# 180 identity products without readers at low priority, and two PSUM banks in place of four for the first attention

## The chip, the cores and the metric

The kernel runs on one core of a Trainium2 chip. The metric is the device time of one execution in microseconds (us). Engines are named as in the profile: PE is the matrix engine, PEld its weight loads, DVE the vector engine, ACT the scalar engine, POOL the GpSimd engine, and SP the engine whose queue issues most DMAs.

## The reference

```
def sm_attn(qq, kk, vv):
    s = scale * np.matmul(qq, kk.transpose(0, 1, 3, 2))
    s = s - np.max(s, axis=-1, keepdims=True)
    a = np.exp(s)
    a = a / (np.sum(a, axis=-1, keepdims=True) + 1e-09)
    return np.matmul(a, vv)
p_packed = sm_attn(p, k, v)
out = sm_attn(q, p_packed, p_packed)
...
h = x @ w_in
sp = np.maximum(h, 0.0) + np.log1p(np.exp(-np.abs(h)))
g = h * erf(sp)
return (g @ w_out).astype(np.float32)
```

There are 8 batches of 8 heads, 576 tokens and a head size of 64. 32 packed queries attend to all tokens (first attention step), and all tokens then attend to the 32 packed results (second step). The outputs, 4608 tokens of 512 features, go through a gated layer with 2048 hidden features. w_in (512 x 2048) and w_out (2048 x 512) arrive as 64-bit floats.

## The kernel before, in words

**Attention per batch.** `attention(b)` is a generator of 12 stages. It loads p, k, v and q of a batch, computes the first scores (L165, tiles s), their maximum and exponential (L170, L174), normalizes (L179), transposes the attention with identity products (L186 and L192, tiles t and p), multiplies with v (L198) and copies the packed result to `pt` (L203). The second scores (L212) are transposed and normalized on DVE and ACT (L215 to L229) and split into a high part `a2h` (ACT, L232) and a low part `a2l` (DVE, L233). Attention of batch b+1 runs beside the units of batch b.

**Folded weights.** `w_prime(b, j)` multiplies `pt` with a quarter of w_in (L243), and ACT and DVE write the product as a high and a low part, `wph` (L245) and `wpl` (L246). So the hidden features need no product of their own with the attention output.

**Units.** A unit is half the tokens of a batch (c = 0 or 1) and one of 8 blocks of 256 hidden features (i). `h_block` makes the hidden block with 12 products of 128x288 into two banks of PSUM (L264; pool `ps_h` with two buffers), copies it with ACT (L267), and passes it through ACT and DVE in turn: L270, L271, L272 on ACT, L273 and L274 on DVE, L275 on ACT, and on DVE the last product, which gives `g` (L280). `o_block` runs three units later (LAG = 3) and adds g times w_out into four PSUM banks, `ps_o0` to `ps_o3` (L308). In the first 12 units (WHOLE) g is one 32-bit tile and each product with w_out is written once; later it is split in parts. A product of two 32-bit tiles counts as two instructions on PE in the profile.

**Weights in 64 bits.** `load_f32` turns a 128x512 piece of w_in or w_out into 32 bits: a DMA into a staging tile (L83, 512 KB), one pass of ACT (L87) and three of DVE (L88, L89, L90). The staging pool has two buffers, and only six conversions (EARLY) borrow others. The next DMA into a staging buffer is issued when the last pass of DVE over it is done. There are 32 such pieces; `plan` spreads them over the first units, and half of w_in and w_out (16 pieces) fall into the first attention and the first five units.

**What sets the order.** The instructions of each engine are put in order when the kernel is built, by a scheduler with modelled durations. What stands earlier in the program has the higher priority. On the chip each engine runs its list strictly in that order, and waits on semaphores where an input isn't there. In names of tiles with their numbers, h0_0_1_0 is batch 0, half 0, block 1, first of its two banks; hs, t, u and g carry batch, half and block; wos4 is the staging tile of piece 4 of w_out and wo4 the converted piece; wi2_3 is the staging tile of quarter 2 of w_in, piece 3.

**Banks of the first attention.** The attention of batch 0 runs before any unit, so the o banks are free. With `roomy` set, `bank` (L125 to L132) goes round three places: `ps_o0` and `ps_o1`, then `ps_o2` and `ps_o3`, then the shared place `ps_m`. Its pieces in turn are the first scores of both halves of the tokens, the transposes t, the packed result p and the second scores of both halves.

Of the kernel before, what the change touches and what calls it, by code (L numbers as in the profile page):

```python
# [8 lines left out]
F32 = mybir.dt.float32  # L9
# [19 lines left out]
def tile_pack_attention_moe(ctx: ExitStack, tc: tile.TileContext, qT, kT, v, pT, w_in, w_out, outT):  # L29
    nc = tc.nc  # L30
    P = 128
    B, _, NC, S = qT.shape
# [17 lines left out]
    WI_AT = (-1, 1)  # L50
    ATT1 = (0, 2)
    ATT2 = 14
    CONV = 2

    EARLY = ("wpl", "wpl", "wph", "wph", "wpl", "wpl")
# [7 lines left out]
    ps_o = ctx.enter_context(tc.tile_pool(name="ps_o", bufs=1, space=bass.MemoryType.PSUM))  # L63
# [3 lines left out]
    ident = cpool.tile([P, P], F32, name="ident")  # L67
# [24 lines left out]
    def load_w_in(j, c, **slot):  # L92
        load_f32(w_in_sb[:, c, j * FB:(j + 1) * FB], w_in[c * P:(c + 1) * P, j * FB:(j + 1) * FB], f"wi{j}_{c}", **slot)

    def load_w_out(f, **slot):
        made = opool.tile([P, DM], F32, name=f"wo{f}", tag="wo")
        load_f32(made[:], w_out[f * P:(f + 1) * P, :], f"wos{f}", **slot)
        wo[f] = made

    def split_w_out(f):  # L100
        hi = opool.tile([P, DM], F32R, name=f"woh{f}", tag="wo")
        lo = opool.tile([P, DM], F32R, name=f"wol{f}", tag="wo")
        nc.scalar.copy(hi[:], wo[f][:])
        nc.vector.tensor_tensor(lo[:], wo[f][:], hi[:], op=ALU.subtract)
        wo_hi[f], wo_lo[f] = hi, lo
# [8 lines left out]
    def attention(b, roomy=False):  # L114
# [3 lines left out]
        turn = [0]  # L118
# [6 lines left out]
        def bank(name):  # L125

            turn[0] += 1
            if roomy and turn[0] % 3:
                d = turn[0] % 3 * 2 - 2
                return [ps_o.tile([P, 512], F32, name=f"{name}_{b}_{x}", tag=f"ps_o{d + x}")[:] for x in range(2)], None  # L130
            ps = ps_m.tile([P, 2, 512], F32, name=f"{name}_{b}", tag="ps_m")
            return [ps[:, 0, :], ps[:, 1, :]], ps  # L132

# [17 lines left out]
        for j in range(NCH):  # L151
            n = min(P, S - j * P)
# [8 lines left out]
        for c2 in range(2):  # L161
            banks = bank(f"s1_{c2}")
            for c in range(NC):
                for r in range(2):
                    nc.tensor.matmul(banks[0][r][NK * c:NK * c + NK, 0:HT], p[64 * r:64 * r + 64, c, :],  # L165
                                     k[c][64 * r:64 * r + 64, c2 * HT:(c2 + 1) * HT], start=True, stop=True)
            copy_out(a1[:, :, c2 * HT:(c2 + 1) * HT], banks, HT)
            yield
# [11 lines left out]
        yield  # L180
        a1t = apool.tile([P, NCH, 2, P], F32, name=f"a1t{b}", tag="big")
        banks = bank("t1")
        for j in range(NT):
            for r in range(2):
                o = (j % 2 * 2 + r) * P
                nc.tensor.transpose(banks[0][j // 2][:, o:o + P], a1[:, r, j * P:(j + 1) * P], ident[:])  # L186
        copy_out(a1t[:, 0:NT].rearrange("p (x j) r k -> p x (j r k)", x=2), banks, 512)
        yield
        banks = bank("p")
        po, pr = banks[0]  # L190
        for r in range(2):
            nc.tensor.transpose(pr[0:REM, r * P:(r + 1) * P], a1[:, r, NT * P:S], ident[:])  # L192
        nc.scalar.copy(a1t[0:REM, NT].rearrange("p r k -> p (r k)"), pr[0:REM, 0:2 * P])
        for j in range(NCH):
            n = min(P, S - j * P)
# [41 lines left out]
    def w_prime(b, j):  # L237
        hi = wpool.tile([P, 2, FB], F32R, name=f"wph{b}_{j}", tag="wph")
        lo = wpool.tile([P, 2, FB], F32R, name=f"wpl{b}_{j}", tag="wpl")
        ps = ps_m.tile([P, 2, 512], F32, name=f"wp{b}_{j}", tag="ps_m")  # L240
        for c in range(NC):
            for r in range(2):
                nc.tensor.matmul(ps[NK * c:NK * c + NK, r, :], pt[b][64 * r:64 * r + 64, NK * c:NK * c + NK],  # L243
                                 w_in_sb[64 * r:64 * r + 64, c, j * FB:(j + 1) * FB], start=True, stop=True)
        nc.scalar.copy(hi[:], ps[:])  # L245
        nc.vector.tensor_tensor(lo[:], ps[:], hi[:], op=ALU.subtract)  # L246
        wp[b, j] = (hi, lo)
# [46 lines left out]
    def o_block(b, c, i, first, last):  # L294

        g = gs.pop((b, c, i))
        t0 = b * S + c * HT
        if first:
            acc[b, c] = []
            for d in range(NDM):  # L300
                po = ps_o.tile([P, 512], F32, name=f"o{b}_{c}_{i}_{d}", tag=f"ps_o{d}")
                acc[b, c].append(po)
        for d in range(NDM):
            for k in range(2):
                f = 2 * i + k
                terms = [(wo, g[0])] if len(g) == 1 else [(wo_hi, g[0]), (wo_hi, g[1]), (wo_lo, g[0])]
                for n, (w, gg) in enumerate(terms):
                    nc.tensor.matmul(acc[b, c][d][:, 0:HT], w[f][:, d * P:(d + 1) * P], gg[:, k, :],  # L308
                                     start=(first and k == 0 and n == 0),
                                     stop=(last and k == 1 and n == len(terms) - 1))  # L310
        if not last:
            return
        for d in range(NDM):
            ob = tpool.tile([P, HT], F32, name=f"ob{b}_{c}_{i}_{d}", tag="ob", bufs=NDM)
            nc.scalar.copy(ob[:], acc[b, c][d][:, 0:HT])
            where = outT[d * P:(d + 1) * P, t0:t0 + HT]
            if (b, c) in begun:
                nc.gpsimd.dma_start(where, ob[:], accum_op=ALU.add)
            else:
                nc.sync.dma_start(where, ob[:])  # L320
        begun.add((b, c))
# [15 lines left out]
    def at(n):  # L337
        return plan.setdefault(n, [])
# [10 lines left out]
    for ph, lists in conv.items():  # L349
# [4 lines left out]
        else:  # L354
            flat = [it for items in lists for it in items]
            n0, n1 = (2 * NB0 * TURNS[p] for p in (ph - 1, ph))
            for k, it in enumerate(flat):
                at(n0 + CONV + k * (n1 - n0 - 2 * CONV) // len(flat)).append(it)
    ready, whole_w = {0: -1}, {}

    def plan_attention(b):
        free = last_of[b - 2] + 1 if b > 1 else 0
        start, end = ATT1 if b == 1 else (free, free + 6)
        if b == NB0 and b > 1:
            start, end = ATT2, first_use[b] - 2
        end = max(free, min(end, first_use[b] - 2))
# [10 lines left out]
    for k, (b, j) in enumerate(uses):  # L377
        if b not in ready:
            plan_attention(b)
        n = ready[b]  # L380
        if k >= NFB:
            n = max(n, last_use[uses[k - NFB]])
        n = max([n] + [m for m, its in plan.items() if any(it[0] == "wi" and it[1] == j for it in its)])
# [10 lines left out]
    def do(items):  # L394
        for it in items:
            if it[0] == "att":
                b = it[1]
                if b not in gens:
                    gens[b] = attention(b)
                next(gens[b])  # L400
            elif it[0] == "sp":
                split_w_out(it[1])
            elif it[0] in ("wi", "wo"):
                conversions[0] += 1
                slot = {}
                if 2 < conversions[0] <= 2 + len(EARLY):
                    slot = dict(pool=wpool, tag=EARLY[conversions[0] - 3])
                if it[0] == "wi":
                    load_w_in(it[1], it[2], **slot)
                else:  # L410
                    load_w_out(it[1], **slot)
            elif it[1:] == (0, 0):
                with tc.high_priority():
                    w_prime(0, 0)
            else:
                w_prime(it[1], it[2])

    first = attention(0, roomy=True)
    early = plan.pop(-1, [])
    next(first)  # L420
# [8 lines left out]
    for n in range(len(units) + LAG):  # L429
        if n < len(units):  # L430
            h_block(*units[n][:3], n < WHOLE)
            do(plan.pop(n, []))
        if n >= LAG:
            o_block(*units[n - LAG])

# [37 lines left out]
```

## Time and profile before

| | us |
|---|---|
| median of 3 runs | 792.65 (790.92 to 794.25) |
| the profiled execution | 789.89 |
| its span | 788.1 |
| PE busy | 744.6 (94%) |
| DVE busy | 599.7 (76%) |
| ACT busy | 597.6 (76%) |

The profiled execution has 1.8 us around its span. Times in a timeline are counted from the start of the span. A row of the timeline has start, duration, engine, line, operation, tiles (written from read), shape and count, and in brackets the idle time of the engine before it and what ended it. A row of the table of stretches has the stretch, its length, the busy time of PE, PEld, DVE, ACT and POOL with instruction counts, the granted clock of PE as a share of full speed, the DMA share and GB/s. The granted clock comes from records of its changes; before the first record, at 8.52 us, the table has no record and writes 1.00.

### The profile page before, as it was taken

The numbers are of one execution on the slowest core, as the hardware profiler recorded it, in microseconds if no ns is written. First come the engines' busy times: TensorE is split into PE (matmuls) and PEld (weight loads), VectorE is DVE, ScalarE is ACT, GpSimd is POOL, SyncE is SP. The second block draws the span as 40 slices with busy tenths as digits, with TensorE's granted clock in tenths as the row PEclk, the third lists the DMA queues.
The fourth block names the chain that finished last, engine by engine and source line by source line (L and its number), as shares of the span: only waits on it lengthen the run. The fifth ranks groups of instructions, "written<-read, shape, count | busy, mean of one in ns | idle before, by whom it ended". The sixth has DMA issues, their size and how long they took to land.

```text
span 788.1 us, 15219 instructions
## 1 busy us (share of the span) xinstructions
PE 744.6 (94%) x6256; PEld 664.1 (84%) x6256; DVE 599.7 (76%) x916; ACT 597.6 (76%) x1011; POOL 15.1 (2%) x22
## 2 busy tenths in 40 slices
PE   3549988999999999999999999999999999999998
PEld 2228756899998898899799998889888998899998
DVE  3887898977689678867887769767886769766664
ACT  3357778988689878887687868778687867878784
POOL 0000000000111100000000000000000000000000
PEclk8568999999999999999999999999999999999999
DMA  8834735002542422013200222002300210000000
GB/s 306 291 110 149 243 116 162 31 17 67 107 88 31 83 76 89 1 39 98 80 32 1 83 81 72 13 1 80 132 32 1 79 47 1 31 2 31 1 31 31
DMA packets 31813, 58.39 MB, mean 74 GB/s; under 512 B 3584, under 2 KB 14848, under 8 KB 31744
## 3 DMA queue, kind: packets, MB, share of 16 engines
q1 hardware_dynamic: 29440, 55.06, 21.5%
q0 software_dynamic: 2304, 2.36, 2.6%
q8 instruction: 49, 0.80, 0.4%
q14 instruction: 20, 0.16, 0.1%
HBM read 45.61 MB, written 11.80 MB: 73 GB/s over the span
## 4 chain that ended last, share of the span: by engine, by line
PE 82%; DVE 7%; DMA 6%; ACT 3%; issue 1%; SPq 0%; ACTq 0%
PE o L308 50%; PE h L264 24%; PE wp L243 4%; DMA wi<-w_in 4%; DMA wos<-w_out 2%; PE p L198 2%; PE s L212 1%; PE s L165 1%; PE t L186 1%; DVE w_in_sb L89 1%; ACT t L270 1%; DVE wo L89 1%; ACT wo L87 1%; DVE w_in_sb L90 1%; DVE g L280 0%
## 5 line engine op out<-in xcount | busy, mean ns | idle before, releaser
L308 PE MATMUL o<-gl,woh 128*128 128x288 f32 x928 | 273.3, 295 | 0.0
L308 PE MATMUL o<-gh,woh 128*128 128x288 f32 x928 | 273.1, 300 | 0.0
L308 PE MATMUL o<-gh,wol 128*128 128x288 f32 x928 | 272.9, 295 | 0.0
L308 PEld LDWEIGHTS o<-gh,woh 128*128 128x128 f32 x928 | 172.1, 187 | 25.5 <-DVE t L273 8.9
L308 PEld LDWEIGHTS o<-gl,woh 128*128 128x128 f32 x928 | 174.3, 188 | 1.8 <-issue 1.3
L308 PEld LDWEIGHTS o<-gh,wol 128*128 128x128 f32 x928 | 174.6, 188 | 1.5 <-issue 1.3
L267 ACT ACTIVATE hs<-h 128x288 f32<-128x288 f32 x256 | 103.2, 412 | 95.4 <-PE h L264 94.6
L264 PE MATMUL h<-a2h,wph 128*128 128x288 f32 x512 | 155.2, 304 | 10.6 <-ACT wph L245 5.9
L264 PE MATMUL h<-a2l,wph 128*128 128x288 f32 x512 | 152.7, 298 | 1.8 <-DVE a2l L233 1.8
L264 PE MATMUL h<-a2h,wpl 128*128 128x288 f32 x512 | 152.6, 298 | 0.0
L283 DVE SCALAR_TENSOR_TENSOR hs<-t,hs 128x576 f32<-128x576 f32 x116 | 87.7, 756 | 72.5 <-ACT t L275 72.5
L275 ACT ACTIVATE t<-t,bias 128x576 f32<-128x576 f32 x128 | 98.8, 772 | 25.3 <-DVE t L274 25.0
L264 PEld LDWEIGHTS h<-a2h,wph 128*128 128x128 f32 x512 | 97.2, 190 | 22.3 <-ACT wph L245 6.8
L273 DVE SCALAR_TENSOR_TENSOR t<-t,hs 128x576 f32<-128x576 f32 x128 | 95.9, 750 | 20.1 <-ACT u L272 19.8
L270 ACT ACTIVATE t<-hs,bias 128x576 f32<-128x576 f32 x128 | 99.6, 778 | 2.9
L271 ACT ACTIVATE t<-t,bias 128x576 f32<-128x576 f32 x128 | 99.3, 775 | 2.3
L264 PEld LDWEIGHTS h<-a2l,wph 128*128 128x128 f32 x512 | 97.4, 190 | 4.3 <-DVE a2l L233 2.8
L272 ACT ACTIVATE u<-t,bias 128x576 f32<-128x576 f32 x128 | 99.3, 776 | 1.8
L264 PEld LDWEIGHTS h<-a2h,wpl 128*128 128x128 f32 x512 | 97.3, 190 | 1.9 <-issue 1.9
L274 DVE SCALAR_TENSOR_TENSOR t<-u,t 128x576 f32<-128x576 f32 x128 | 96.3, 752 | 1.6
L287 DVE TENSOR_TENSOR gl<-hs,gh 128x576 fp32r<-128x576 f32 x116 | 87.3, 753 | 1.5
L286 DVE CAST gh<-hs 128x576 fp32r<-128x576 f32 x116 | 52.9, 456 | 35.0 <-PE o L308 33.8
(60 smaller groups left out, 637.3 us busy)
## 6 DMA issues: line engine op xcount, KB each, us to landing
k<-kT SPq DMA_DIRECT2D x32, 288.0 KB, 4.3
q<-qT SPq DMA_DIRECT2D x32, 288.0 KB, 4.3
outT<-ob SPq DMA_DIRECT2D x64, 144.0 KB, 1.8
wi<-w_in SPq DMA_DIRECT2D x16, 512.0 KB, 6.0
v<-v SPq DMA_DIRECT2D x32, 256.0 KB, 3.6
wos<-w_out SPq DMA_DIRECT2D x16, 512.0 KB, 3.6
outT<-ob POOLq DMA_DIRECT2D x16, 144.0 KB, 3.7
v<-v SPq DMA_DIRECT2D x8, 128.0 KB, 4.2
```

What stands on the lines that cost most here:

```text
L264: nc.tensor.matmul(ps[:, 0:HT], w[:, r, fo:fo + P], a[:, r, c * HT:(c + 1) * HT], start=(n == 0), stop=(n == 5))
L267: nc.scalar.mul(hs[:, k, :], ps[:, 0:HT], 0.5)
L270: nc.scalar.activation(t[:], hs[:], AF.Tanh, bias=bias[:, 0:1], scale=2.0 * T_SCALE)
L271: nc.scalar.activation(t[:], t[:], AF.Square, bias=bias[:, 1:2], scale=Q_SCALE)
L272: nc.scalar.activation(u[:], t[:], AF.Tanh, bias=bias[:, 2:3], scale=U_SCALE)
L273: nc.vector.scalar_tensor_tensor(t[:], t[:], 0.5 * A2, hs[:], op0=ALU.mult, op1=ALU.add)
L274: nc.vector.scalar_tensor_tensor(t[:], u[:], 0.5 * A1, t[:], op0=ALU.mult, op1=ALU.add)
L275: nc.scalar.activation(t[:], t[:], AF.Tanh, bias=bias[:, 3:4], scale=2.0 * A_SCALE)
L283: nc.vector.scalar_tensor_tensor(hs[:], t[:], 1.0, hs[:], op0=ALU.add, op1=ALU.mult)
L286: nc.vector.tensor_copy(ghi[:], hs[:])
L287: nc.vector.tensor_tensor(glo[:], hs[:], ghi[:], op=ALU.subtract)
L308: nc.tensor.matmul(acc[b, c][d][:, 0:HT], w[f][:, d * P:(d + 1) * P], gg[:, k, :], start=(first and k == 0 and n == 0), stop=(last and k = ...
```

## The change

There are two edits. `bank` goes round two places instead of three: `ps_o0` and `ps_o1`, then `ps_m`. And after the hidden block of unit 0 and the plan's work of that unit, `keep_busy` writes 180 products of the 128x128 identity with itself into a tile in `ps_o3`. Nothing reads that tile.

```
+    BUSY = 180
...
         def bank(name):
             turn[0] += 1
-            if roomy and turn[0] % 3:
-                d = turn[0] % 3 * 2 - 2
-                return [ps_o.tile([P, 512], F32, name=f"{name}_{b}_{x}", tag=f"ps_o{d + x}")[:] for x in range(2)], None
+            if roomy and turn[0] % 2:
+                return [ps_o.tile([P, 512], F32, name=f"{name}_{b}_{x}", tag=f"ps_o{x}")[:] for x in range(2)], None
...
+    def keep_busy():
+
+        idle = ps_o.tile([P, P], F32, name="idle", tag="ps_o3")
+        for _ in range(BUSY):
+            nc.tensor.matmul(idle[:], ident[:], ident[:], start=True, stop=True)
...
         if n < len(units):
             h_block(*units[n][:3], n < WHOLE)
             do(plan.pop(n, []))
+        if n == 0:
+            keep_busy()
         if n >= LAG:
             o_block(*units[n - LAG])
```

In the program the products stand behind the first attention and unit 0, and ahead of unit 1; the scheduler puts them into PE's list in ten groups. In PE's order they are: 13 ahead of the first scores, 36 ahead of the transposes t, 15 ahead of the products with v, 13 ahead of the second scores, 14 ahead of the first folded weights, then 21, 17, 1 and 6 around the first scores of batch 1 and the start of unit 0, and 44 between unit 0 and unit 1. Lines behind the new constant have numbers one higher in the changed kernel, up to `bank`.

On PE, between unit 0 and unit 1 (h0_0_0 and h0_0_1), the list before has no step between the two hidden blocks:

```order
L264 MATMUL h0_0_0_1_299<-a2h0_273,wph0_0_277 128x288
L264 MATMUL h0_0_0_1_299<-a2l0_274,wph0_0_277 128x288
L264 MATMUL h0_0_0_1_299<-a2h0_273,wpl0_0_278 128x288
L264 MATMUL h0_0_1_0_377<-a2h0_273,wph0_0_277 128x288
L264 MATMUL h0_0_1_0_377<-a2l0_274,wph0_0_277 128x288
```

The same place on PE in the changed kernel:

```order
L264 MATMUL h0_0_0_1_298<-a2h0_272,wph0_0_276 128x288
L264 MATMUL h0_0_0_1_298<-a2l0_273,wph0_0_276 128x288
L264 MATMUL h0_0_0_1_298<-a2h0_272,wpl0_0_277 128x288
L422 MATMUL idle_375<-ident_82 128x128 x44
L264 MATMUL h0_0_1_0_557<-a2h0_272,wph0_0_276 128x288
L264 MATMUL h0_0_1_0_557<-a2l0_273,wph0_0_276 128x288
```

The last 44 products now stand between the units. Behind unit 1 the folded weights wp0_1 come next in both lists; behind those, the first out products (L308) now stand ahead of unit 2 and its neighbours, where they stood behind them.

On ACT, at the copies of unit 1 out of PSUM (hs0_0_1) and the high part of the second folded weights (wph0_1), before:

```order
L267 ACTIVATE hs0_0_1_376<-h0_0_1_0_377 128x288
L87 ACTIVATE w_in_sb_84<-wi2_0_579 128x512
L272 ACTIVATE u0_0_0_308<-t0_0_0_307,bias_83 128x576
L174 ACTIVATE a1_1_345,sm1_369<-a1_1_345,m1_366 128x576 x2
L267 ACTIVATE hs0_0_1_376<-h0_0_1_1_385 128x288
L87 ACTIVATE w_in_sb_84<-wi2_1_585 128x512
L245 CAST wph0_1_441<-wp0_1_443 128x1024
```

The same place on ACT in the changed kernel:

```order
L88 ACTIVATE w_in_sb_84<-wi2_1_765 128x512
L275 ACTIVATE t0_0_0_306<-t0_0_0_306,bias_83 128x576
L88 ACTIVATE wo4_834<-wos4_835 128x512
L267 ACTIVATE hs0_0_1_556<-h0_0_1_0_557 128x288
L267 ACTIVATE hs0_0_1_556<-h0_0_1_1_565 128x288
L270 ACTIVATE t0_0_1_573<-hs0_0_1_556,bias_83 128x576
L271 ACTIVATE t0_0_1_573<-t0_0_1_573,bias_83 128x576
L88 ACTIVATE wo5_841<-wos5_842 128x512
L245 CAST wph0_1_621<-wp0_1_623 128x1024
```

The copies of unit 1 have moved behind the conversion of wo4, and wph0_1 behind that of wo5.

On ACT, at the last step of unit 2 (L275 of t0_0_2) and the conversion of wi2_3, before:

```order
L87 ACTIVATE wo6_713<-wos6_714 128x512
L267 ACTIVATE hs0_0_3_627<-h0_0_3_0_628 128x288
L275 ACTIVATE t0_0_2_555<-t0_0_2_555,bias_83 128x576
L267 ACTIVATE hs0_0_3_627<-h0_0_3_1_636 128x288
L270 ACTIVATE t0_0_3_644<-hs0_0_3_627,bias_83 128x576
L271 ACTIVATE t0_0_3_644<-t0_0_3_644,bias_83 128x576
L272 ACTIVATE u0_0_3_645<-t0_0_3_644,bias_83 128x576
L87 ACTIVATE wo7_720<-wos7_721 128x512
L87 ACTIVATE w_in_sb_84<-wi2_3_727 128x512
```

The same place on ACT in the changed kernel:

```order
L88 ACTIVATE wo7_900<-wos7_901 128x512
L272 ACTIVATE u0_0_2_736<-t0_0_2_735,bias_83 128x576
L270 ACTIVATE t0_0_3_824<-hs0_0_3_807,bias_83 128x576
L271 ACTIVATE t0_0_3_824<-t0_0_3_824,bias_83 128x576
L88 ACTIVATE w_in_sb_84<-wi2_3_907 128x512
L272 ACTIVATE u0_0_3_825<-t0_0_3_824,bias_83 128x576
L275 ACTIVATE t0_0_2_735<-t0_0_2_735,bias_83 128x576
L267 ACTIVATE hs0_1_0_866<-h0_1_0_0_867 128x288
```

L275 of unit 2, on which g0_0_2 waits, has moved behind the conversion of wi2_3. In the later stages the lists of PE, ACT and DVE differ in places up to about the twenty-second unit, and are then alike.

## The prediction

> **What bounds the kernel now.** I began with the chain of work that ended last, then the table of stretches, and then followed PE's waits back through the timelines of ACT and DVE. First the chain by engine, from the page:
>
> ```profile
> PE 82%; DVE 7%; DMA 6%; ACT 3%; issue 1%; SPq 0%; ACTq 0%
> ```
>
> The split is one of time: the table of stretches shows PE without a gap from about 138 us to 771 us, at full clock. Columns are the stretch, length, busy time of PE, PEld, DVE, ACT, POOL, then granted clock, DMA share and GB/s.
>
> ```profile
> 9.32:46.34 37.02, 14.34 (x173) 8.12 (x173) 29.20 (x50) 15.88 (x27) 0.00 (x0) 0.53 0.74 264
> 52.89:56.30 3.41, 0.00 (x0) 0.00 (x0) 1.46 (x3) 2.18 (x5) 0.00 (x0) 0.99 0.23 95
> 56.30:66.54 10.24, 6.79 (x24) 5.99 (x25) 9.58 (x19) 8.50 (x15) 0.00 (x0) 0.50 0.34 109
> 66.54:104.09 37.55, 37.42 (x283) 28.45 (x281) 30.86 (x51) 28.34 (x49) 0.00 (x0) 1.00 0.65 210
> 104.09:107.50 3.41, 1.64 (x18) 0.67 (x19) 3.41 (x7) 3.21 (x5) 0.00 (x0) 0.99 0.00 0
> 107.50:110.92 3.42, 3.42 (x9) 2.36 (x7) 3.42 (x6) 1.53 (x2) 0.00 (x0) 0.51 0.56 169
> 114.33:117.74 3.41, 2.24 (x17) 1.75 (x10) 3.41 (x7) 2.67 (x4) 0.00 (x0) 1.00 0.00 0
> 124.57:138.22 13.65, 11.55 (x73) 8.34 (x74) 12.77 (x21) 13.62 (x25) 0.00 (x0) 1.00 0.37 118
> 138.22:771.00 632.78, 632.78 (x5432) 581.77 (x5433) 485.13 (x728) 506.08 (x857) 14.39 (x16) 1.00 0.17 48
> ```
>
> So the change can move the end only by what it moves on PE up to about 138 us: from there the same products follow back to back in both kernels. Until 46 us PE is idle most of the time; until 66.5 us it mostly runs at half clock; from 66.5 to 104 us it is full; from 104 to 138 us it waits now and then on DVE and ACT, which are full. The chain within the first 120 us holds these pieces (start, length, what):
>
> ```profile
> 57.31 3.90 DMA wos<-w_out
> 61.70 3.45 DMA wos<-w_out
> 75.63 5.71 DMA wi<-w_in
> 118.96 3.92 DMA wi<-w_in
> ```
>
> These are loads of weights into the two staging buffers. Each waits until DVE is through with the buffer's last piece, then ACT and DVE convert it. PE speed is hardly in this chain.
>
> **The price of one product.** No identity product stands in the trace. The nearest rows are the transposes, of the same 128x128 shape and weights of the same width: 8 of them in 1.03 us at full clock, 7 in 1.70 us at half clock.
>
> ```profile
> 192.55 1.03 PE L186 MATMUL t<-ident,a 128*128 128x128 f32 x8
> 16.80 1.70 PE L186 MATMUL t<-ident,a 128*128 128x128 f32 x7
> ```
>
> The length of one, first to last, is told by the view of the tile (least, median, most in ns):
>
> ```profile
> L186 PE MATMUL t<-ident,a x64: 270/273/473, 16.4 to 632.3; 128*128 128x128 f32 x64
> ```
>
> Less the 0.27 us that the last of the 8 takes, 7 steps in 0.76 us are 0.109 us each. At half clock, less up to 0.47 us, 6 steps in 1.23 us are 0.205 us or a little more. An identity product is a 32-bit product, and these count as two instructions: 0.22 us at full clock, 0.43 us at half (between twice 0.205 and twice 0.22), 39 us or 77 us for all 180. If it were one instruction, half of that; I take two.
>
> **The 13 products ahead of the first scores.** Loads of weights for these scores come in steps of 0.48 us; the last row is the end of the identity on POOL:
>
> ```profile
> 6.76 0.18 PEld L165 LDWEIGHTS s<-k,p 64*32 64x32 f32 x2 [0.30 <-issue]
> 7.24 0.18 PEld L165 LDWEIGHTS s<-k,p 64*32 64x32 f32 x2 [0.30 <-issue]
> 7.91 0.19 PEld L165 LDWEIGHTS s<-k,p 64*32 64x32 f32 x4 [0.49 <-DMA k<-kT]
> 1.02 0.29 POOL masks.py:199 TENSOR_SCALAR_AFFINE_SELECT ident<-ident 128x128 f32<-128x128 f32 x1
> ```
>
> An out product of the same 288 columns steps by about 0.25 us at full clock (16 in 4.04 us, a row at 78.57 us below). So PE is at half clock here, though the table writes 1.00 before its first record. The 13 products take 13 x 0.43 = 5.6 us, or 2.9 us at full clock. The last piece of k, at 7.91 us, covers them either way: POOL has the identity ready at 1.3 us, and 1.3 + 5.6 = 6.9 us. Uncovered they would push the scores, first begun at 4.25 us, back by 2.7 us. Price: 0.
>
> **The 123 products before unit 0, and the two banks.** 36 + 15 + 13 + 14 + 21 + 17 + 1 + 6 = 123 products, 27 us at full clock. The stretch 9.32 to 46.34 us of the table runs from the end of the first scores to unit 0:
>
> ```profile
> 4.25 5.07 PE L165 MATMUL s<-k,p 64*32 64x288 f32 x32 [4.25 <-DMA k<-kT]
> 46.34 0.61 PE L264 MATMUL h<-a2l,wph 128*128 128x288 f32 x1 [1.81 <-DVE a2l L233]
> 50.59 0.29 PE L264 MATMUL h<-a2h,wpl 128*128 128x288 f32 x1
> ```
>
> PE works 14.34 of its 37.02 us, nearly all at half clock, so some 7 us at full clock. 27 + 7 = 34 us fit into 37. The cover is DMA and DVE, which set the pace (DMA share 0.74, DVE 29.20 us); without it the products would cost their 27 us. Of the banks, the second half of the scores and the packed result move into `ps_m`, whose earlier reader is done at each turn, and ACT copies the transposes in two pieces, which I price at nothing, since `pt` waits for a piece of w_in in DVE's new order. That wait makes the first attention later, and fewer conversions of w_out ahead of a2l make it earlier. I take 0 for this part, within -1 and +1 us.
>
> **The 44 products between units 0 and 1.** A hidden block of 12 products takes 85.92 - 84.22 = 1.7 us at full clock (rows below). Unit 0 has ten products left at 46.3 us and ends near 46.3 + 1.4 = 47.7 us, the 44 products take 44 x 0.22 = 9.7 us, and unit 1 ends at 59.1 us; before, its last product began at 50.59 us. ACT waits for unit 1, and its copies now stand behind the conversion of wo4. These are ACT's rows for wph0_1, wo4, wo5 and wi2_3:
>
> ```profile
> 57.72 0.99 ACT L245 CAST wph<-wp 128x1024 fp32r<-128x1024 f32 x1
> 61.23 0.68 ACT L87 ACTIVATE wo<-wos 128x512 f32<-128x512 f32 x1 [0.52 <-DMA wos<-w_out]
> 65.17 0.67 ACT L87 ACTIVATE wo<-wos 128x512 f32<-128x512 f32 x1 [0.71 <-DMA wos<-w_out]
> 81.37 0.67 ACT L87 ACTIVATE w_in_sb<-wi 128x512 f32<-128x512 f32 x1 [3.29 <-DMA wi<-w_in]
> ```
>
> wo4 is through at 61.9 us, so 2.8 us of cover remain beyond the 44 products: price 0. At half clock they would take 9.5 us more and stick out by 6.7 us.
>
> **Unit 2.** wph0_1 now stands behind wo5: 65.17 + 0.67 + 0.99 = 66.8 us in place of 58.7 us, 8.1 us later. PE's rows, with those for the next part:
>
> ```profile
> 58.76 0.61 PE L264 MATMUL h<-a2h,wph 128*128 128x288 f32 x1 [5.87 <-ACT wph L245]
> 69.50 0.38 PE L192 MATMUL p<-ident,a 128*64 128x128 f32 x2
> 78.57 4.04 PE L308 MATMUL o<-g,wo 128*128 128x288 f32 x16
> 82.54 1.74 PE L212 MATMUL s<-q,pt 64*32 64x288 f32 x16
> 84.22 0.40 PE L264 MATMUL h<-a2h,wph 128*128 128x288 f32 x1
> 85.92 4.53 PE L308 MATMUL o<-g,wo 128*128 128x288 f32 x18
> ```
>
> From 58.76 to 69.50 us PE did unit 2, 8 transposes and 16 out products, mostly at half clock. In the new order the out products run ahead of unit 2, while PE waits for wph0_1. Behind 66.8 us only unit 2 (1.7 us) and the transposes (0.9 us) are left: 69.4 us, level with before. The gain of the clock, half of the 6.79 us that PE worked at half clock from 56.30 to 66.54 us, is spent on waiting for ACT. The Trainium skill has a rule that speaks for the change here (TensorE: Matmul & The Clock Gate, section Why this matters for your kernels): keep PE busy for 4 us and leave no gap of about 3 us, and products run at full rate. By it alone the sum would lose 3.4 us at this place; by the rows above, which put wph0_1 behind wo5, it loses nothing. PE then stands idle for some 3 us before 66.8 us; the stretch at 104.09 us, with 1.64 of 3.41 us busy, was followed by half clock, that at 114.33 us, with 2.24 us, was not. If the clock drops, unit 2 and the transposes take 2.6 us more; so 0 to +2.6 us here, which the next wait swallows.
>
> **Unit 2's g.** L275 of unit 2 now stands behind wi2_3. From ACT's row at 81.37 us: 0.67 us for the conversion, 0.78 us for L272 of unit 3 (the page's mean, below), as much for L275 of unit 2, of the same size, and 0.76 us for g on DVE. So g0_0_2 is ready at 84.4 us; before, it was begun at 74.19 us:
>
> ```profile
> 74.19 0.76 DVE L280 SCALAR_TENSOR_TENSOR g<-t,hs 128x576 f32<-128x576 f32 x1
> ```
>
> ```profile
> L272 ACT ACTIVATE u<-t,bias 128x576 f32<-128x576 f32 x128 | 99.3, 776 | 1.8
> ```
>
> The 16 out products on g (4.04 us) and the second scores (up to 1.74 us) then end at 90.2 us, where before they were done at 84.22 us: 5.9 us late. If wi2_3 lands in 3.9 us, like the load at 118.96 us, instead of 5.7, and the buffer comes 1 us sooner, and the scores need half, it is 2.2 us. I take 4.0, the middle: no row is nearer to one end.
>
> **104 to 138 us.** PE's waits from 100 to 140 us:
>
> ```profile
> PE wp L243 <- DVE wpl L246: 2.3, 2, 1.8
> PE o L308 <- DVE g L280: 1.8, 2, 1.2
> PE wp L243 <- DVE w_in_sb L90: 1.4, 1, 1.4
> PE h L264 <- ACT hs L267: 0.5, 2, 0.3
> ```
>
> The first and third, 3.7 us, end with folded and converted weights, whose chain of buffers is not later than before; they can swallow lag. The waits for g and hs move with the lag. On the other side ACT is full (13.62 of 13.65 us from 124.57), and there its new list has wo12 and wo13 ahead of steps of the first unit of batch 1 that stood ahead of them: at least 2 x 0.67 = 1.3 us. Net: 4.0 - 3.7 + 1.3 = +1.6 us.
>
> **The sum.** 0 for the products and banks, 0 for unit 2, and 1.6 us. The profiled execution took 789.89 us (span 788.1 and 1.8 around it), so 791.5 us. The median of the runs is 792.65 us, 2.8 us above it; the same step gives 794.3 us.
>
> **Rivals.** *Faster.* If the loads land soon enough that PE is not held, the half clock of the two stretches goes: half of 6.79 and of 3.42 us, 5.1 us in all, from the median 787.5 us. For it: PE is full from 66.54 to 104.09, so what it gets done earlier counts. Against it: the new orders of ACT put units 1 and 2 behind loads. The rows show that the clock follows gaps (none busy from 52.89, then half clock at 56.30 us); the trace agrees with the rule named above so far, and whether the time follows the clock is what is open. *Slower by the 44 products.* A dip in PE's work ahead of them drops the clock, and they stick out by 6.7 us: with the 1.6 us, 8.3 us, 801.0 us. It decides if they take over 0.28 us each (9.7 + 2.8 over 44). *Slower by g.* The 5.9 us are carried in full, with 1.3 us: 7.2 us, 799.9 us. It holds if g0_0_2 comes after 84 us and PE has no wait left to lose. *The products don't lift the clock.* 123 x 0.43 + 14.3 = 67 us in place of 37 us: some 30 us, 822 us. Against it: the clock rose at 66.54 us behind products of the same full height and width.
>
> **Chances.** The forecast 0.46, within 3.5 us of itself (790.8 to 797.8); faster 0.23; the 44 products 0.15; g 0.13; no lift 0.03. A measurement of this kernel can tell about 0.5%, 4 us, from no change. Of the forecast 0.01 falls below that; so faster 0.24, the same 0.45, slower 0.31. The range runs from the faster rival to the 44 products, 787.5 to 801.0 us, and leaves out about 2 in 10: the last rival and the outer halves of the two at its ends.
>
> **What would show it.** The table of stretches should read full clock from within the first 9 us to about 63 us, with PE near full. The 44 products should take about 9.7 us; ACT's L267 of unit 1 should follow the conversion of wo4, not wait for PE; wph0_1 should be made after 65 us; g0_0_2 should follow wi2_3. If PE waits at 57 to 66 us for nothing of the kind and its rows at 104 us come some us earlier, the forecast is wrong on the fast side; if ACT waits for PE at unit 1, on the slow side.

## The result, and the profile after

The changed kernel takes 797.39 us (median of 6 runs, 795.8 to 798.58) beside 791.7 us before (790.86 to 794.25): a ratio of 1.0068, 95% interval 1.005 to 1.0085. It is slower by 5.4 us (0.0068 of 791.7), inside the forecast's range, 3.1 us above the forecast. The forecast had put it 1.6 us above the time before, so it missed most of the rise; part of that doesn't show in the 3.1 us, since before stands 0.95 us lower by its 6 runs than by the 3 that the forecast started from (792.65). The profiled execution took 798.58 us (span 796.8), 1.2 us above its median; that of before stood 1.8 us below its own, so the two traces lie 8.7 us apart where the medians lie 5.7.

The chain by engine, from the page after:

```profile
PE 82%; DMA 7%; DVE 6%; ACT 3%; issue 1%; SPq 1%; DVEq 0%
```

The table of stretches after, cut as that of before was:

```profile
9.32:46.34 37.02, 35.48 (x415) 32.07 (x414) 27.93 (x46) 15.85 (x27) 0.00 (x0) 1.00 0.75 261
...
56.30:66.54 10.24, 8.38 (x60) 6.19 (x58) 7.04 (x15) 5.73 (x13) 0.00 (x0) 1.00 0.35 105
...
107.50:110.92 3.42, 0.00 (x0) 0.00 (x0) 3.42 (x5) 3.42 (x8) 0.00 (x0) 0.93 0.07 14
114.33:117.74 3.41, 3.41 (x9) 2.40 (x8) 3.41 (x5) 2.01 (x3) 0.00 (x0) 0.57 0.37 133
124.57:138.22 13.65, 8.61 (x63) 5.09 (x61) 9.17 (x15) 10.23 (x20) 0.00 (x0) 0.86 0.64 183
138.22:771.00 632.78, 632.50 (x5421) 581.35 (x5414) 484.56 (x727) 507.14 (x858) 14.39 (x16) 1.00 0.17 49
```

The share of the chain says nothing new; the stretches do. Until 66.5 us PE now has full clock, and to 46 us it is busy 35.48 of 37.02 us where it was busy 14.34. From 138 us on all is as it was. In between, in 124.57 to 138.22, PE has lost 2.9 us of work (8.61 for 11.55), and a stretch of 3.42 us near 108 us is empty. PE's rows at the places of the prediction (in brackets the wait ahead of a row and what ended it):

```profile
1.36 4.71 PE L422 MATMUL idle<-ident 128*128 128x128 f32 x26 [1.36 <-POOL ident masks.py:199]
5.99 1.16 PE L165 MATMUL s<-k,p 64*32 64x288 f32 x16
7.86 1.16 PE L165 MATMUL s<-k,p 64*32 64x288 f32 x16 [0.71 <-DMA k<-kT]
48.02 9.98 PE L422 MATMUL idle<-ident 128*128 128x128 f32 x88
67.40 0.40 PE L264 MATMUL h<-a2h,wph 128*128 128x288 f32 x1 [2.72 <-ACT wph L245]
...
111.38 1.96 PE L243 MATMUL wp<-w_in_sb,pt 64*32 64x512 f32 x16 [4.55 <-DVE wpl L246]
135.16 0.61 PE L264 MATMUL h<-a2h,wph 128*128 128x288 f32 x1 [4.41 <-ACT hs L267]
```

A product counts as two instructions, so the 44 are the 88 of 9.98 us. The last two rows are the new waits: 4.55 us for wpl, where there were 1.8 us at 105.86, and 4.41 us for hs, where there were 0.3 and 0.2. And ACT's rows on which they and the steps of the forecast rest:

```profile
63.02 0.67 ACT L88 ACTIVATE wo<-wos 128x512 f32<-128x512 f32 x1 [4.45 <-DMA wos<-w_out]
63.59 0.69 ACT L267 ACTIVATE hs<-h 128x288 f32<-128x288 f32 x2
66.35 0.99 ACT L245 CAST wph<-wp 128x1024 fp32r<-128x1024 f32 x1
79.44 0.69 ACT L88 ACTIVATE w_in_sb<-wi 128x512 f32<-128x512 f32 x1 [0.24 <-DMA wi<-w_in]
80.70 0.76 ACT L275 ACTIVATE t<-t,bias 128x576 f32<-128x576 f32 x1
105.89 0.66 ACT L88 ACTIVATE w_in_sb<-wi 128x512 f32<-128x512 f32 x1 [2.54 <-DMA wi<-w_in]
107.51 0.99 ACT L245 CAST wph<-wp 128x1024 fp32r<-128x1024 f32 x1
128.48 0.67 ACT L88 ACTIVATE wo<-wos 128x512 f32<-128x512 f32 x1 [1.31 <-DMA wos<-w_out]
132.06 0.66 ACT L88 ACTIVATE wo<-wos 128x512 f32<-128x512 f32 x1 [1.00 <-DMA wos<-w_out]
134.70 0.71 ACT L267 ACTIVATE hs<-h 128x288 f32<-128x288 f32 x2
```

L245 at 107.51 makes the wph from which wpl is taken; it stands behind the conversion of w_in at 105.89, which waited 2.54 us for its load. Before, it stood ahead of it (101.64 and 103.04 us). The copies of hs at 134.70 stand behind wo13 at 132.06, which waited for its load too.

### The profile page after: what moved, and what is told of

It reads as the page before. It is cut to its first block, busy times and chain, and to the rows that moved or that the text cites. A ratio compares the mean times of both kernels' runs of the same rounds, so it can differ in the third digit from the quotient of the medians.

```text
span 796.8 us, 15936 instructions
## 1 busy us (share of the span) xinstructions
PE 776.5 (97%) x6616; PEld 700.7 (88%) x6616; DVE 600.9 (75%) x916; ACT 597.7 (75%) x1011; POOL 15.1 (2%) x22
## 4 chain that ended last, share of the span: by engine, by line
PE 82%; DMA 7%; DVE 6%; ACT 3%; issue 1%; SPq 1%; DVEq 0%
PE o L308 49%; PE h L264 24%; DMA wi<-w_in 4%; PE wp L243 4%; DMA wos<-w_out 2%; PE p L198 2%; PE s L212 1%; PE s L165 1%; PE t L186 1%; DMA q<-qT 1%; ACT w_in_sb L88 1%; DVE w_in_sb L90 1%; DVE wo L91 1%; DVE w_in_sb L91 1%; DVE w_in_sb L89 0%
## 5 line engine op out<-in xcount | busy, mean ns | idle before, releaser
L308 PE MATMUL o<-gh,woh 128*128 128x288 f32 x928 | 274.0, 300 | 0.0
L308 PE MATMUL o<-gl,woh 128*128 128x288 f32 x928 | 273.3, 295 | 0.0
L308 PE MATMUL o<-gh,wol 128*128 128x288 f32 x928 | 273.1, 295 | 0.0
L308 PEld LDWEIGHTS o<-gh,woh 128*128 128x128 f32 x928 | 172.4, 187 | 25.9 <-DVE t L273 8.9
L308 PEld LDWEIGHTS o<-gh,wol 128*128 128x128 f32 x928 | 174.6, 188 | 1.5 <-issue 1.3
L308 PEld LDWEIGHTS o<-gl,woh 128*128 128x128 f32 x928 | 174.3, 188 | 1.3 <-issue 1.3
L275 ACT ACTIVATE t<-t,bias 128x576 f32<-128x576 f32 x128 | 98.6, 770 | 25.6 <-DVE t L274 25.2
L273 DVE SCALAR_TENSOR_TENSOR t<-t,hs 128x576 f32<-128x576 f32 x128 | 96.0, 750 | 18.5 <-ACT u L272 18.3
```

The source lines that it names most:

```text
L273: nc.vector.scalar_tensor_tensor(t[:], t[:], 0.5 * A2, hs[:], op0=ALU.mult, op1=ALU.add)
L275: nc.scalar.activation(t[:], t[:], AF.Tanh, bias=bias[:, 3:4], scale=2.0 * A_SCALE)
```

## The experiments

At first I held that the new orders of ACT, DVE and SP cost the time, and the products none (theory A). The rival was PE's time in the 44 products between units 0 and 1 (theory B). The orders can be held fixed while products go: the list of instructions is edited after the scheduler is done. A product that neither waits nor signals is dropped; it has no reader, so nothing else changes.

```diff
+    for block in nc.main_func.blocks:
+        seen, kept = 0, []
+        for ins in block.instructions:
+            idle = "idle" in str(ins)
+            seen += idle
+            if not (idle and DROP and not ins.has_wait() and not ins.has_update()):
+                kept.append(ins)
+        block.instructions = kept
     r = _run(nc, [arrays], core_ids=[0])
```

`seen` numbers the products in PE's order: 1 to 13 stand ahead of the first scores, 14 to 49 from there to the transposes at 17 to 19 us, 50 to 136 from there into unit 0, 137 to 180 between units 0 and 1. The first waits and the last signals, so they stay in every kernel made in this way. All ratios are to the kernel before on the same chip, with 95% intervals; 0.001 is 0.8 us.

**The orders without the products** (`DROP` is `True`).

> The changed kernel with its orders on every engine exactly as they are, but 178 of the 180 identity products taken out of PE's stream after the orders were fixed (two stay: the first, which waits, and the last, which signals). Theory A, the new orders of ACT, DVE and SP cost the time, not the products: the median stays near that of the changed kernel, 796 to 799 us (against 791.7 before), and the waits for wpl near 107 us and for hs near 131 us are both there, 4 us each. Theory B, the PE time of the 44 products between units 0 and 1 costs it: 791 to 793 us. Theory C, the products' full clock is worth time that the orders lose again: over 800 us.

792.82 us, ratio 1.0023 (1.0009 to 1.0037). Theory A falls in the main, and so does theory C: the orders by themselves cost 1.8 us, and the products make up the rest. Yet PE's waits from 100 to 140 us stay:

```profile
PE h L264 <- ACT hs L267: 4.2, 1, 4.2
PE wp L243 <- DVE wpl L246: 3.3, 1, 3.3
```

So these two waits belong to the orders. They look dear (7.5 us for 2.8 before), but all that the orders do comes to 1.8 us.

**Without the 44** (`DROP` is `seen > 136`).

> As the changed kernel, but of the products only the first 136 and the last one remain; the 43 others between units 0 and 1 are taken out after the orders were fixed. Theory A (orders): 796 to 799 us, since unit 1's copies on ACT wait for the conversion of wo4 at 63 us with or without the 44 products. Theory B (PE time of the 44): 790 to 793 us.

795.4 us, ratio 1.0047 (1.0029 to 1.0065): between the theories. The products ahead of unit 0 cost something that neither of them has.

**The two banks alone** (`BUSY = 0`).

> The two PSUM banks without any product (BUSY = 0); the orders are the scheduler's own for this kernel and near those of before. Theory A: within 2 us of before, 790 to 794 us. A rival, that the two banks by themselves make the first attention later: 795 us or more, and unit 0 begins over 2 us later than 46.3 us.

790.7 us, ratio 0.9993 (0.9978 to 1.0008): the banks cost nothing.

**90 products** (`BUSY = 90`).

> The change with 90 products in place of 180: all 90 stand ahead of unit 0, none is left over for between units 0 and 1, and ACT's order is close to that of before. Theory A: no loss, 789 to 793 us. If the clock that the products lift is worth time (the faster rival): 787 us or less. If products ahead of unit 0 cost PE time: 795 us or more.

793.95 us, ratio 1.0033 (1.0021 to 1.0046): no gain and some loss, between the cases of the expectation, in an order close to that of before.

From the chain of the run without the 44 came the next theory. PE's own queue is on it, with the products:

```profile
20.18 3.35 PE idle L422 x30
...
34.68 4.88 PE idle L422 x42
40.21 3.99 PE idle L422 x34
```

Theory E: PE runs its list in order, and batches that are longer than the wait they stand in hold up the step behind them. Theory D: the 13 products ahead of the first scores cost, since these begin at 5.99 in place of 4.25 us.

**Only the first 13** (`DROP` is `seen > 13`), **only 14 to 136** (`seen <= 13 or seen > 136`), **only the 44** (`seen <= 136`), **and the kernel of 90 less its first 13** (`seen <= 13`).

> The changed kernel's orders on every engine; of its products only the 13 ahead of the first scores (and the last one, which signals) remain. Theory D, these 13 cost the time because the first scores begin at 6 to 6.7 us in place of 4.2 us: 794.5 to 795.5 us, most of what the first 136 products cost (795.4 with them, 792.8 without). Theory E, the products that stand in PE's queue from 17 to 47 us cost it, because batches of them are longer than the waits that they fill: 792 to 793.5 us.

> The changed kernel's orders; the products 14 to 136 remain, those ahead of the first scores (but for one) and those between units 0 and 1 (but for the last) are taken out. Theory D (the 13): 792 to 793.5 us. Theory E (batches longer than the waits in PE's queue): 795 to 796 us, and the second scores and unit 0 begin 2 us later than without products (37.1 and 41.8 us).

> The changed kernel's orders; only the 44 products between units 0 and 1 remain (and the first one, which waits). If the 44 cost time of their own (797.4 with all, 795.4 without the 44): 794.5 to 796 us. As forecast (they lie beside the load of wo4): 792 to 793.5 us.

> The kernel with 90 products and the orders near those of before, less the products ahead of the first scores (but for one). Theory D: 790 to 791.5 us, as with the two banks alone (790.7). Theory E: 793 to 794.5 us, as with all 90 (793.95). If full clock from 9 to 37 us is worth time once the 13 are gone: under 789.5 us.

Only the 13: 792.95 us, 1.0023 (1.001 to 1.0035), exactly as without any. Only 14 to 136: 796.32 us, 1.007 (1.0046 to 1.0093). Only the 44: 794.31 us, 1.0045 (1.0028 to 1.0062). 90 less 13: 794.38 us, 1.0042 (1.0025 to 1.0058). Theory D falls. With 14 to 136 unit 0 begins at 43.85 us, as theory E expected. The cost sits in products 14 to 136, and some 1.7 us in the 44 (1.0045 less 1.0023 alone, and 1.0068 less 1.0047 beside the others: each no larger than its uncertainty, but twice the same).

Then 14 to 136 were parted. Theory F, from the start of the traces: beside products the loads of 4 to 20 us come later.

**Only 14 to 49** (`not 13 < seen <= 49`), **only 50 to 136** (`not 49 < seen <= 136`), **every third of 50 to 136** (`not (49 < seen <= 136 and seen % 3 == 0)`).

> The changed kernel's orders; only the 36 products that stand behind the first scores (9 to 17 us, while the loads fill the DMA engines) remain, with the first one and the last. Theory E (batches in PE's queue from 17 us on are longer than the waits): 792 to 793.5 us, as without products. Theory F, the products cost because the loads of 4 to 20 us come later beside them: 794 to 795.5 us, and the fifth load of w_in is issued after 18.3 us (17.2 to 18.0 us in the kernels without them).

> The changed kernel's orders; only the 87 products from 17 us to unit 0 remain (and the first one and the last). Theory E: 794.5 to 796 us, and unit 0 begins 2 us later than without them (41.7 us). Theory F: 792 to 793.5 us.

> As the run with the 87 products from 17 us to unit 0, but with every third of them only, so that a batch takes 1.1 us (2.2 at half clock) where it took 3.3. Theory E: the batches fit into the waits and the cost is gone, 792 to 793.5 us. If each product costs the same wherever it stands: a third of what the 87 cost.

The 36: 796.24 us, 1.0061 (1.0046 to 1.0076). The 87: 796.54 us, 1.0065 (1.0045 to 1.0086). The 29: 793.28 us, 1.0019 (1.0007 to 1.003), as without any; a third of what the 87 cost over the orders would make it 1.0037. Theory E expected nothing of the 36 and theory F nothing of the 87; each of the two groups alone costs some 3 us over the orders, and both together no more (1.007). The traces show two ways to be late.

In the trace of the 36 the lag comes with the loads. ACT in the run without products, and then with the 36: the fourth piece of w_in, for which it waits, and behind it in its list the copies of the transposes:

```profile
19.99 0.67 ACT L88 ACTIVATE w_in_sb<-wi 128x512 f32<-128x512 f32 x1 [0.66 <-DMA wi<-w_in]
20.56 1.07 ACT L141 COPY a1t<-t 128x512 f32<-128x512 f32 x2
```

```profile
22.70 0.66 ACT L88 ACTIVATE w_in_sb<-wi 128x512 f32<-128x512 f32 x1 [0.69 <-DMA wi<-w_in]
23.27 1.05 ACT L141 COPY a1t<-t 128x512 f32<-128x512 f32 x2
```

Both are 2.7 us later, and PE, which has no product left to do there, waits. Its rows without products, and with the 36:

```profile
21.92 4.63 PE L198 MATMUL p<-a1t,v 128*64 128x32 f32 x80 [1.63 <-ACT a1t L193]
27.32 2.17 PE L212 MATMUL s<-q,pt 64*32 64x288 f32 x32 [0.76 <-DVE pt L203]
30.68 1.96 PE L243 MATMUL wp<-w_in_sb,pt 64*32 64x512 f32 x16 [1.19 <-DVE ta L215]
37.08 1.22 PE L165 MATMUL s<-k,p 64*32 64x288 f32 x16 [4.44 <-DVE wpl L246]
41.78 0.85 PE L264 MATMUL h<-a2h,wph 128*128 128x288 f32 x2 [3.49 <-ACT a2h L232]
```

```profile
24.62 3.76 PE L198 MATMUL p<-a1t,v 128*64 128x32 f32 x80 [4.02 <-ACT a1t L193]
44.37 0.85 PE L264 MATMUL h<-a2h,wph 128*128 128x288 f32 x2 [3.49 <-ACT a2h L232]
```

Unit 0 begins 2.6 us later, with the same wait ahead of it: the whole chain has moved.

That the 36 made the loads late is shown in its direction only. Of the 2.7 us, 0.7 stood already at the first piece of w_in (ACT began to convert it at 10.13 us for 9.40), ahead of the first of the 36 at 10.46 us. The other 2.0 came between the first piece and the fourth: 12.57 us for 10.59. In the runs with these orders this distance is 10.59 to 10.77 us in the five without products at 9 to 17 us, and 10.79, 11.07, 11.69 and 12.57 us in the four with them, so its size differs from one profile to the next. The sign that theory F named is no clearer: the fifth load was issued at 18.58 us, after 18.3, but also at 18.21 us with the 87, which leave 9 to 17 us empty. The 3 us of the 36 are measured over 6 executions; that they pass through the loads is argued from one profile.

The 87 act through PE's queue. Nothing lifts the clock for them at first: 30 instructions take 4.60 us where the run with 14 to 136 took 3.51 in the same place. PE's rows with the 87:

```profile
20.86 4.60 PE L422 MATMUL idle<-ident 128*128 128x128 f32 x30
25.39 2.64 PE L198 MATMUL p<-a1t,v 128*64 128x32 f32 x80
27.96 3.17 PE L422 MATMUL idle<-ident 128*128 128x128 f32 x26
31.06 1.20 PE L212 MATMUL s<-q,pt 64*32 64x288 f32 x32
32.19 3.39 PE L422 MATMUL idle<-ident 128*128 128x128 f32 x28
35.51 1.09 PE L243 MATMUL wp<-w_in_sb,pt 64*32 64x512 f32 x16
36.53 4.96 PE L422 MATMUL idle<-ident 128*128 128x128 f32 x42
41.42 0.71 PE L165 MATMUL s<-k,p 64*32 64x288 f32 x16
42.06 4.06 PE L422 MATMUL idle<-ident 128*128 128x128 f32 x34
45.88 0.51 PE L264 MATMUL h<-a2h,wph 128*128 128x288 f32 x2
```

and ACT's copy that L198 needs:

```profile
22.29 0.37 ACT L193 COPY a1t<-p 64x256 f32<-64x256 f32 x1
```

It was done at 22.66 us; L198 began at 25.39. No row of these has a wait, which is how a queue that has become the bound looks: the step is late and nothing is named. The waits of the run without products, shown above, are 1.63, 0.76, 1.19, 4.44 and 3.49 us; into them go batches of 4.60, 3.17, 3.39, 4.96 and 4.06 us. Full clock makes the steps between shorter (4.63 to 2.64 us, 2.17 to 1.20), but not by as much, and unit 0 begins 4.1 us late. Of these, 0.6 us stood before: the first batch begins at 20.86 us, where the transposes were through at 20.29 without products. The other 3.5 arise in PE's queue (25.0 us from there to unit 0 for 21.5). With every third product only, waits are back and the lag is 0.5 us:

```profile
20.56 1.63 PE L422 MATMUL idle<-ident 128*128 128x128 f32 x10
22.43 2.64 PE L198 MATMUL p<-a1t,v 128*64 128x32 f32 x80 [0.23 <-ACT a1t L193]
...
42.26 0.85 PE L264 MATMUL h<-a2h,wph 128*128 128x288 f32 x2 [1.24 <-ACT a2h L232]
```

These lags at unit 0 go on to the stages that set the end. Unit 2 begins at 64.83 us without products, 64.82 with the 29, 66.96 with the 36 and 67.70 with the 87. The folded weights behind the wait for wpl begin at 107.06, 107.34, 110.38 and 111.19 us.

Why the two groups don't add up is argued here and not tried apart: with the 36 ahead of them, the 87 run at full clock from the start, and what they still hold up is hidden in part by the loads' lag. In the changed kernel unit 0 begins at 43.96 us, 2.2 us behind the run without products.

**The orders of 90** (`BUSY = 90`, `DROP` is `True`).

> The kernel with 90 products and its orders, with all products but one taken out after the orders were fixed. If its time (793.95 with the 90, 794.38 without the 13 ahead of the scores) is that of its orders: 793.5 us or more. If the products in PE's queue make it: 790 to 791.5 us, as with the two banks alone (790.7).

791.11 us, ratio 0.9997 (0.9983 to 1.001). In this order too the products make the loss: 1.0033 and 1.0042 with them, nothing without.

**What stays open.** For the 44 no place was found. In the profile with them alone unit 2 begins 0.5 us behind the run without products (65.36 for 64.83), about what its first loads had lost before unit 0 (ACT began to convert the third piece 0.6 us later, 19.27 for 18.66). The rest comes at 76 to 128 us, where three loads take longer. Two of them, without products, and with the 44:

```profile
76.52 4.60 DMA wos<-w_out
...
96.06 5.47 DMA wi<-w_in
```

```profile
76.75 5.39 DMA wos<-w_out
...
96.72 6.02 DMA wi<-w_in
```

The third was issued at 120.35 us without products and at 121.55 us with the 44. ACT's conversion of it, without and with:

```profile
123.86 0.66 ACT L88 ACTIVATE wo<-wos 128x512 f32<-128x512 f32 x1 [1.26 <-DMA wos<-w_out]
```

```profile
127.00 0.66 ACT L88 ACTIVATE wo<-wos 128x512 f32<-128x512 f32 x1 [3.30 <-DMA wos<-w_out]
```

Whether the products do that, 20 to 70 us after they are through, or whether this execution differed in it by chance, one profile each can't say; it took 795.87 us, 1.6 us above the median of its kernel. Moving the two conversions of w_out back behind the copies of hs, which might take the 4.4 us wait away, was not tried. Nor were the products of the order of 90 parted any further.

## Why the prediction was right and where not

The time fell into the range, but the forecast of 794.3 us was 3.1 us short: what was put at no change that can be told came out slower by more than 0.5%, the case that had 0.31. That it fell into the range is in part luck, since two terms that were put at nothing, both of products, make most of the loss.

- **The bound.** Right: 632.50 of 632.78 us busy behind 138 us, and what differs is decided before.
- **The price of a product.** Right: 88 instructions in 9.98 us are 0.113 us each, 0.23 us a product for 0.22.
- **The 13 ahead of the scores.** Right: covered by the last k; with them alone the time is that without (1.0023 and 1.0023). They were through in 4.7 us for 5.6: 0.18 us an instruction, between the 0.113 of full clock and the 0.205 of half, so the clock rose on the way.
- **The 123 products before unit 0.** This is the main step that failed: "34 us fit into 37", price 0. With the products 1 to 136 over the orders alone it is 1.9 us (1.0047 less 1.0023), with 14 to 136 it is 3.7, and the two intervals overlap. The sum was right, 35.48 us busy in that stretch, but fitting a sum into a sum is not enough: a product fits only into the wait in which it stands, and waits of 0.8 to 4.4 us were given batches of 3.2 to 5 us. And the cover, "DMA and DVE set the pace", was taken as given, where in the profiles the loads came later with the products beside them (ACT began to convert the fourth piece of w_in at 20.9 to 22.7 us in the six kernels with products at 9 to 17 us, at 19.8 to 20.8 us in the seven others of the runs); how much of that the products made stays open.
- **The banks.** Right: 0.9993.
- **The 44.** Their place and length were right (9.98 us for 9.7; ACT's copies at 63.59 right behind wo4). Price 0 was not, as far as can be told: 1.7 us alone, no larger than its uncertainty, from a cause that stays open. The rival that they stick out at half clock was wrong in its mechanism: they ran at full clock.
- **Unit 2.** Right: wph0_1 was cast at 66.35, through at 67.34, for 66.8; PE had waited 2.72 us for it, and the clock fell (0.67 in the mean from 68.3 to 71.7 us), the second of the two cases.
- **Unit 2's g.** Its order was right, its size by luck. g0_0_2 followed wi2_3 (79.44, L275 at 80.70), and the second scores ended at 88.3 us where they had ended at 84.28, 4.0 us late as taken. But the 4.0 were to come from the order, and in the run with the orders alone the scores ended at 85.19 us (84.48 and 0.71), 0.9 us late: the other 3.1 came with the products, whose lag was put at nothing. There wi2_3 was converted at 76.82 us, 4.5 us ahead of the 81.37 of before, where the sum's early case had 2.8 us. With the orders alone PE then came to the wait for wpl at 103.75 us (107.06 less 3.31), where it had come to it at 104.06, and in the changed kernel at 106.83.
- **104 to 138 us.** Wrong in its terms: 3.7 us were to be swallowed, and the wait for wpl grew to 4.55 us instead, for wph had come to stand behind a conversion that waits for its load. And 1.3 us for wo12 and wo13 counted ACT's busy time alone, not the 1.31 and 1.00 us in which ACT stood still for their loads. These errors and that of g offset one another: the orders cost 1.8 us measured, 1.6 forecast, and that agreement is luck.
- **The faster rival.** Wrong on the time, right on the clock. In the stretches from 9.32 to 46.34 and from 56.30 to 66.54 us the granted clock was 1.00, as the rule of the Trainium skill has it (TensorE: Matmul & The Clock Gate, section Why this matters for your kernels); the trace agrees with it there. Right behind them it is stricter than the rule: the wait of 2.72 us ahead of unit 2, under the rule's gap of about 3 us, and one of 0.63 us soon after were followed by half clock. The worth of the clock is seen where unit 0 and unit 1 follow each other. In the run without the 44, unit 0 began 2.2 us behind the run with the orders alone (43.95 for 41.78), and unit 1 ended 0.15 us ahead of it (49.98 for 50.13). Most of that the clock made good: from the first product with a2l to the end of unit 1 took 3.4 us (46.62 to 49.98) for 5.2 (44.98 to 50.13). Unit 2, which waits for ACT, began 1.8 us behind again (66.67 for 64.83). No run has the full clock without the products, so what the clock alone is worth stays open.

## What to carry to other kernels

Filler on an in-order engine cost time here where a batch was longer than the very wait it stood in; compare it wait by wait, not sum by sum, and look for steps that begin late with no wait in front of them. A faster clock helps only where that engine sets the end; here full clock on the first 66 us, with the filler that brought it, gained nothing. To tell the price of an instruction from the price of the order that it leaves behind, take the instruction out after the order is fixed.

## What the runs showed of the hardware

- With PE full from 9 to 17 us ACT began to convert the fourth load, for which it waited, 1.4 us later on the mean (21.8 us over six kernels, 20.4 over seven), and 0.4 us of that stood at the first load already (10.0 and 9.6 us). The DMA share read 1.04 to 1.05 in all. The rate in 8.5 to 17.5 us was 349 to 368 GB/s with products and 359 to 375 without, so the two overlap; why the loads come later no run tells.
- Behind the wait of 4.55 us for wpl, the stretch of 114.33 to 117.74 us above reads 0.57 with PE full: a late wait put half clock upon work that is then on the path.
- A granted clock without a record is no measurement. With the 44 alone the table writes 1.00 for 9.32 to 46.34 us, as it does ahead of a first record, but the products of unit 0 follow each other there in 0.24 us, where they take 0.13 at full clock.
